# Windowed attention and a low-rank mixer: the same products in another planned order

## The chip, the cores and the metric

The kernel runs on one core of one Trainium2 chip. The metric is device time in microseconds; the kernel before has a median of 240.48 us over 8 runs (239.02 to 241.27). TensorE (PE) multiplies matrices into PSUM, VectorE (DVE), ScalarE (ACT) and GpSimd (POOL) work elementwise, and SyncE (SP) and GpSimd issue transfers (DMA). Each of these executes its own list of instructions in order.

## The reference

```python
# q, k, v: (4, 8, 768, 64); n_global 8, n_local 96
scores = q @ k.T / 8 + bias          # bias = -slope[h] * distance; kept: 0 <= i - j < 96, or j < 8
x = softmax(scores) @ v              # then (4, 768, 512): tokens by channels
u = x + (x.T @ U @ V).T              # mixes tokens through rank 32
out = u + relu(u @ w_ch1) @ w_ch2    # 512 -> 2048 -> 512
```

## The kernel before, in words

The work is cut into 16 **pairs** (batch b of 4, two heads at a time; pair p = 4b + hp) and 4 **mixers**, one for each batch, which follow its four pairs.

A pair is a chain of tasks; the digit after the letters is the pair:

- `lk`, `lq`, `lv` load K, Q and V with a cast to fp16. GpSimd issues them (L393 to L401), except pair 0's K and Q, which SP loads as fp32 and `Ck0`, `Cq0` cast. Three buffers each for K and Q, four for V.
- `TK`, `TQ` transpose K and Q on TensorE (L538) for pairs 0 to 6, evacuated by `EK` (ScalarE) and `EQ`; from pair 7 on `EK` and `EQ` are DMA transposes on SP's queue (L562). `KO` copies the global keys beside each block.
- `VO` makes a copy of V shifted by 32 rows, `VG` adds the global rows. `CFG['VO']` says who shifts: `P`, GpSimd in three copies `VOp.0` to `VOp.2` (L308), for pairs 0 and 1; `S`, one transfer on SP's queue (L589), for all others. `VG` is always GpSimd's.
- `SB` (batch 0 alone) writes the bias into PSUM, `S` adds the scores (L646), in up to three steps; `EX` takes the exponent (ScalarE, L673), `MK` multiplies by a mask (batches 1 to 3; L682, L686).
- `PV` multiplies with V (L734, L735); `RC` and `NM` normalize into `x_sb` (L769, L773); `XC` casts it to fp16 (GpSimd, L799, except for a batch's last pair); `UP` transposes x and multiplies by U (L713, L718); `TE` evacuates the second (L807); `HM` adds the V factor of the mixer (L813); `E0` (for the last pair of a batch `E0` and `E1`) evacuates the sum as one quarter of u, transposed. The last pair of batch 0 does `PV` to `UP` in three parts (`NH` for `NM` and `XC`).

A mixer is 16 steps of `M1a` (three of four quarters of u) and `M1b` (the last) with `RL` (relu, ScalarE, L872) behind them (L855), and then the second product as 7 instead of 8 block products (`P1` to `P7`, L934) for each of three row blocks t: `RS` starts a block (L922), `PA` and `PB` prepare sums of the relu's result on VectorE (L889 to L894), `DI` and `DA` to `DH` gather the results (L947, L970), `O` stores. `w1_0` to `w1_3` and `w2_0` to `w2_3` are quarters of the two weights, loaded once by GpSimd (L443, L452); `TWa` and `TWb` form sums of w2 on VectorE for P4 to P7. `M1a b.n` needs `w1_(n//4)` and u of three pairs.

The order is not written by hand. A `Planner` holds every task with an engine, an assumed duration, a priority, dependencies and buffers, and plays them through: at each step the engine that can start first takes, of its tasks that are ready within a small margin, the one of lowest priority number. The resulting order is then issued; each engine executes its list in that order, waiting where an operand is not there. `PRIO` replaces the priorities of named tasks. Where the plan leaves TensorE a gap ahead of the first mixer, small matmuls on zeros fill it (`idle`, L1005).

Of the kernel before, what the change touches and what calls it, by code (L numbers as in the profile page):

```python
# [16 lines left out]
PE, ACT, DVE, POOL, SP = "PE", "ACT", "DVE", "POOL", "SP"  # L17


PRIO = {  # L20
    "DA0.1": 6761.6, "DB0.1": 7457.2, "DB0.2": 8384.0, "DB1.1": 8060.5, "DB1.2": 7985.3, "DC2.0": 7792.2,
    "DD0.0": 7862.4, "DD0.1": 9270.9, "DD0.2": 8194.4, "DD1.0": 7863.4, "DE0.2": 9402.3, "DF1.2": 9397.4,
    "DG0.0": 8430.4, "DG0.1": 7596.4, "E02": 5865.5, "EQ1": 5461.4, "EQ4": -770.7, "EX13.0": 2425.7,
    "EX7.0": 3812.7, "EX8.0": 3775.7, "HM0": 2046.8, "HM12": 6279.7, "HM4": 6676.8, "HM9": 6950.7,
    "KO2": 5496.8, "KO6": 7318.7, "MK5.1": 9128.9, "NM3": 6024.6, "NM6": 7530.1, "P11.1": 6997.7,
    "P11.2": 1129.7, "P13.0": 1397.9, "P13.1": 5738.6, "P13.2": 5821.2, "P20.1": 6584.3, "P21.2": 7125.0,
    "P22.1": 6477.8, "P22.2": 6901.9, "P31.0": 1661.0, "P31.1": 8414.8, "P31.2": 1130.8, "P32.2": 1563.3,
    "P40.0": 6158.6, "P42.2": 6069.4, "P51.0": 5444.1, "P51.1": 6635.4, "P51.2": 1447.3, "P52.0": 7575.6,
    "P52.2": 6200.8, "P53.0": 6280.2, "P53.1": 6149.2, "P53.2": 6395.6, "P60.1": 1345.9, "P62.0": 6610.3,
    "P62.2": 7609.1, "P63.0": 6108.0, "P63.1": 5480.1, "P63.2": 5772.1, "P70.0": 8347.1, "P70.1": 6738.9,  # L30
    "P70.2": 7027.2, "P71.2": 1364.6, "P72.1": 6440.8, "P73.0": 5851.1, "P73.1": 5567.0, "P73.2": 5452.8,
    "PA0.2": 7917.5, "PV10": 6222.2, "PV4": 6245.6, "PV9": 5349.2, "RS1.1": 6269.9, "RS1.2": 1110.0,
    "RS2.0": 1541.0, "RS2.2": 1422.3, "RS3.1": 5892.6, "RS3.2": 6041.8, "S10.2": 1370.0, "S13.0": 1158.9,
    "S14.2": 6699.6, "S15.2": 6800.7, "S2.0": 1451.2, "S4.0": 7711.3, "S5.2": 6779.7, "S8.0": 5814.4,
    "S9.0": 1264.8, "SB0.0": 1281.0, "TD0": 6084.1, "TE12": 9033.5, "TE4": 7848.7, "TK5": 6104.0,
    "TQ6": 6583.1, "TWa1": 7306.5, "TWb1": 10021.5, "UP10": 1511.1, "UP13": 7260.0, "UP5": 6730.5,
    "UP8": 1455.2, "back": 5375.3, "bias2": 5491.5, "bias5": 5236.3, "bias7": 5097.0, "lk1": -2540.4,
    "lk2": -3457.2, "lk3": -3923.7, "lk4": -38.4, "lk5": 1252.9, "lk6": 1838.7, "lq1": -3379.0,
    "lq2": -3313.7, "lq3": -3230.2, "lq4": -245.4, "lv0": -2414.7, "lv2": -4220.0, "lv4": 502.1,
    "ones0": -3282.3, "ones1": -2613.4, "ones2": -2230.4, "ones3": -2415.2, "vs1": 6166.9, "w1_0": 605.5,  # L40
    "w1_3": 1786.5, "w2_3": 2150.6,
}
CFG = {'petr': (4, 5, 6), 'E': 'DAD', 'VO': 'PPSSSSSSSSSSSSSS'}

# [162 lines left out]
def kernel(  # L207
# [13 lines left out]
    nc = tc.nc  # L221
# [13 lines left out]
    D1 = D + 1  # L235
# [3 lines left out]
    PO = P - 32  # L239
# [6 lines left out]
    def sb(name, shape, dt, n=None):  # L246
        if n is None:
            return cst.tile(shape, dt, name=name)
        return [cst.tile(shape, dt, name=f"{name}{i}") for i in range(n)]
# [9 lines left out]
    vs = sb("vs", [P, 4, HS], FP16)  # L259
# [27 lines left out]
    bias = sA[:, 0]  # L287
# [14 lines left out]
    def copy(eng, dst, src):  # L302
        if eng == ACT:
            nc.scalar.activation(dst, src, AF.Copy)  # L304
        elif eng == DVE:
            nc.vector.tensor_copy(dst, src)
        else:
            nc.gpsimd.tensor_copy(dst, src)  # L308

    def add(eng, dur, prio, fn, deps=(), name="", **kw):  # L310
        return pl.add(name, eng, dur, PRIO.get(name, prio), fn, deps, **kw)
# [32 lines left out]
    c_rel = add(DVE, 2.2, -89, build_rel, [c_id16], name="rel3")  # L344
    c_mask = []

    def bias_of(h, eng):
        def go():
            if eng == ACT:
                nc.scalar.activation(bias[:, h], rel3, AF.Copy, scale=slope[h] / qk_scale)  # L350
            else:
                nc.vector.tensor_scalar_mul(bias[:, h], rel3, slope[h] / qk_scale)
        return go

    c_bias = []
    for h in range(H):
        e = DVE if h in CFG.get("bias_dve", range(H)) else ACT
        c_bias.append(add(e, 0.53 if e == ACT else 0.24, -45 + h if h < 2 else 100 * (h // 2) - 30, bias_of(h, e), [c_rel], name=f"bias{h}"))

    def ones(i):  # L360
        return lambda: nc.gpsimd.memset(vt[i][:, :, :, D:D1], 1.0)
# [114 lines left out]
    def load_mixer():  # L476
# [4 lines left out]
    c_back = add(DVE, 0.07, -44, lambda: nc.vector.memset(uf[0:1, 0, 0:1], 0.0), [c_bias[0]], name="back")  # L481
    c_mixl = add(SP, 0.9, -44, load_mixer, [c_back], size=0.8, parts=2, name="mixl")
    c_u16 = add(
        DVE, 0.95, 10,
        lambda: nc.vector.tensor_copy(u16, uf.unsqueeze(2).broadcast_to((P, NB, RG, R))), [c_mixl], name="u16",
    )

    def build_vs(g):
        def go():
            o, v1, v2 = vs[0:R, g], vf[:, 0:HS], vf[:, HS:S]  # L490
            if g % 2 == 0:
                nc.vector.tensor_copy(o, v2 if g else v1)
            else:
                nc.vector.tensor_tensor(o, *((v2, v1) if g == 1 else (v1, v2)), ALU.subtract)
        return go

    c_vz = add(DVE, 0.5, -95, lambda: nc.vector.memset(vs, 0.0), name="vz")
    c_vs = [add(DVE, 0.5 if g % 2 == 0 else 0.6, 11 + g, build_vs(g), [c_mixl, c_vz], name=f"vs{g}") for g in range(4)]


# [21 lines left out]
    def attention(p):  # L522
        b, hp = pairs[p]
        h0 = 2 * hp
        base = 100 * p
        first = b == 0
        kdur = 0.25
        last = hp == NP - 1
        mg = 0.3 if first else 0.5
        gq, gk, gv, tq, tk, tv = loads[p]  # L530
        gkT, gqT = Group("kT", 2), Group("qT")
        A1, A2 = (ANY1, ANY2) if first else (ATT1, ATT2)
# [35 lines left out]
        if p in by_pe:  # L568
            g1, g2 = Group("ps", among=A1), Group("ps", among=A1)
# [25 lines left out]
        if vm != "S":  # L595
            ve = {"D": DVE, "P": POOL, "A": ACT}[vm]

            def vo_d(c):
                return lambda: copy(ve, vo[gv.slot][c:c + 32], vt[gv.slot][c + 32:c + 64, :, 0:NB - 1])

            VO = [
                add(ve, {POOL: 0.95, DVE: 0.8, ACT: 0.8}[ve], base + 4, vo_d(c), [tv], name=f"VO{p}.{c // 32}") for c in range(0, PO, 32)
            ]
        else:
            VO = [add(SP, 0.6, base + 4, vo_sp, [tv], size=0.6, name=f"VO{p}")]
# [118 lines left out]
        for s in range(3):  # L724
# [12 lines left out]
            if not split:  # L737
# [6 lines left out]
                    rel=[geps[s]] + ([gv] if s == 2 else []), name=f"PV{p}.{s}",  # L744
# [86 lines left out]
        else:  # L831
            e = {"A": ACT, "D": DVE}[CFG.get("E", "DDD")[p] if first else CFG.get("EB", "A")]
# [7 lines left out]
    def mlp(b):  # L840
        base = 100 * NP * (b + 1) + 5000
# [65 lines left out]
        for t in range(ht):  # L907
            gX, gY = Group("ps", 3, among=among), Group("ps", 4, among=among)
            g2, g3 = Group("u2", 2), Group("u3", 1)
# [3 lines left out]
            def half(g, i):  # L913
                return ps[:, g.slot, i * hd:(i + 1) * hd]
# [28 lines left out]
            def dv(eng, dur, fn, dp, nm, **kw):  # L943
                return add(eng, dur, -10, fn, dp, name=f"{nm}{b}.{t}", **kw)

            def plus(e, o, x, y):
                return lambda: e.tensor_tensor(o(), x(), y(), ALU.add)  # L947
# [10 lines left out]
            D1 = dv(DVE, 0.42, plus(V_, lambda g2=g2: u2[g2.slot], lambda gX=gX: half(gX, 1), lambda g2=g2: u2[g2.slot]), [P6, D0], "DA", rel=[gX])  # L958
# [5 lines left out]
            se = POOL if CFG.get("SE", "D") == "P" and not (b == B - 1 and t == ht - 1) else DVE  # L964
# [4 lines left out]
            def both(sn=sn, xy=xy, g2=g2):  # L969
                sn.tensor_tensor(xy, xy, u2[g2.slot].unsqueeze(1).broadcast_to((P, 2, hd)), ALU.add)  # L970

            D5 = dv(se, 1.27 if se == POOL else 0.65, both, [D1], "DE", rel=[g2])
            D6 = dv(DVE, 0.42, plus(V_, lambda x11=x11: x11, lambda gX=gX: half(gX, 0), lambda x11=x11: x11), [P2], "DF", rel=[gX])
            D7 = dv(DVE, 0.42, plus(V_, lambda x21=x21: x21, lambda gY=gY: half(gY, 0), lambda x21=x21: x21), [P4, D5], "DG", rel=[gY])
            D8 = dv(DVE, 0.42, plus(V_, lambda x12=x12: x12, lambda gY=gY: half(gY, 1), lambda x12=x12: x12), [P3, D5], "DH", rel=[gY])

# [10 lines left out]
    for b in range(B):  # L987
        for hp in range(NP):
            if b == 1 and hp == 0:
                c_mask += [  # L990
                    add(
                        ACT, 0.54, 330 + 5 * h,
                        lambda h=h: nc.scalar.activation(mask[:, h], rel3, AF.Exp, scale=slope[h]),
                        [c_rel, pl.names[CFG.get("mask_after", "EX3.1")]], name=f"mask{h}",
                    )
                    for h in range(H)
                ]
            attention(b * NP + hp)
        mlp(b)
# [55 lines left out]
```

The softmax here doesn't subtract the row's maximum and nothing guards it: scores larger than these inputs give would overflow.

## Time and profile before

| | us |
|---|---|
| median of 8 runs | 240.48 |
| the profiled execution | 239.71 |
| its span | 237.9 |
| TensorE busy, all of the span | 226.5 (95%) |
| GpSimd busy | 90.1 (38%) |
| first product of the first mixer starts | 34.76 |
| last matmul ends | 233.92 |
| granted TensorE clock, mean | 0.999 |

A row of the timeline gives start, length, engine, line, operation, tiles and count, and in brackets the idle time ahead of it with what ended it. A row of the stretches gives busy time by engine. "Landing" of a transfer counts from the start of its issue.

### The profile page before, as it was taken

To read this page: it belongs to the slowest core of one execution; us is meant where nothing else is said; L and a number is where in the kernel's file an instruction comes from. 1 tells how busy PE (TensorE), PEld (TensorE's weight loads), DVE (VectorE), ACT (ScalarE), POOL (GpSimd) and SP (SyncE) were. 2 spreads that over 40 slices of the span, in tenths; PEclk is the share of its full clock that TensorE was granted. 3 is DMA by queue.
4 is the path that set the end of the run, shared out by engine and by line. 5 is a ranking of instruction groups with operands and counts; after the bars stand their busy time and mean duration, and the time that the engine had idled before them with its cause. 6 is when DMAs were issued, how large, how long until landed. Compare 5 with 4: busy or idle time off the path is not lost.

```text
span 237.9 us, 5808 instructions
## 1 busy us (share of the span) xinstructions
PE 226.5 (95%) x2436; PEld 165.4 (70%) x2436; DVE 147.5 (62%) x317; ACT 122.8 (52%) x165; POOL 90.1 (38%) x116
## 2 busy tenths in 40 slices
PE   7996989999999999999999999999999999999993
PEld 3653865556888975666888866657889765668872
DVE  6864760548999881656778973465488631537452
ACT  3884955787345246957541358557441225661000
POOL 8759992725959648082074910020001000000000
PEclk9999999999999999999999999999999999999999
DMA  8999699999999999999689999000002220000024
GB/s 178 172 119 130 49 173 197 202 207 187 162 115 155 173 147 170 192 163 132 128 53 162 129 182 174 3 0 0 3 1 91 88 91 2 0 3 0 0 91 176
DMA packets 86442, 26.18 MB, mean 110 GB/s; under 512 B 73840, under 2 KB 83440, under 8 KB 86416
## 3 DMA queue, kind: packets, MB, share of 16 engines
q0 software_dynamic: 63616, 13.24, 70.9%
q1 hardware_dynamic: 22800, 12.57, 25.5%
q8 instruction: 19, 0.31, 0.6%
q14 instruction: 7, 0.06, 0.1%
HBM read 27.46 MB, written 6.29 MB: 142 GB/s over the span
## 4 chain that ended last, share of the span: by engine, by line
PE 81%; DMA 8%; POOL 4%; DVE 3%; issue 1%; SPq 0%; ACT 0%; DVEq 0%; POOLq 0%
PE ps L855 36%; PE ps L934 31%; DMA vt<-in_v_dram 4%; PE ps L646 4%; DMA w<-in_moe_w_ch_dram 3%; PE ps L922 2%; PE ps L735 2%; DMA sA<-in_q_dram 2%; PE ps L713 2%; PE ps L718 2%; PE ps L734 2%; POOL vo L308 2%; PE ps L813 1%; DVE x_sb L947 1%; POOL x L799 1%
## 5 line engine op out<-in xcount | busy, mean ns | idle before, releaser
L855 PE MATMUL ps<-uT,w 128*128 128x384 f16 x512 | 86.4, 327 | 1.5 <-DMA w<-in_moe_w_ch_dram 1.1
L855 PEld LDWEIGHTS <-w 128*128 128x128 f16 x512 | 48.7, 98 | 33.6 <-DMA w<-in_moe_w_ch_dram 1.3
L872 ACT ACTIVATE htr<-ps 128x768 f16<-128x768 f32 x64 | 51.9, 811 | 30.4 <-PE ps L855 30.2
L673 ACT ACTIVATE ep<-ps 128x1024 f16<-128x1024 f32 (+1 forms) x48 | 43.9, 952 | 21.3 <-PE ps L646 21.2
L934 PEld LDWEIGHTS <-htr 128*128 128x128 f16 x384 | 36.6, 98 | 7.0 <-issue 1.5
L934 PEld LDWEIGHTS <-sA 128*128 128x128 f16 x288 | 27.7, 98 | 4.9 <-issue 0.9
L889 DVE TENSOR_TENSOR sA<-htr 128x768 f16<-128x768 f16 x16 | 8.9, 557 | 30.6 <-ACT htr L872 30.6
L401 POOL DMA_DIRECT2D vt<-in_v_dram x16 | 16.8, 1048 | 28.3 <-PE ps L735 24.2
L947 DVE TENSOR_TENSOR x_sb<-ps,x_sb 128x256 f32<-128x256 f32 x48 | 19.4, 419 | 12.8 <-PE ps L934 12.1
L934 PE MATMUL ps<-tB,htr 128*128 128x256 f16 x192 | 24.7, 273 | 1.1 <-DVE x_sb L947 1.0
L934 PE MATMUL ps<-w,sA 128*128 128x256 f16 x192 | 24.5, 273 | 0.8 <-DVE x_sb L947 0.5
L799 POOL CAST x<-x_sb 128x768 f16<-128x768 f32 x12 | 10.8, 898 | 37.8 <-DVE x_sb L773 37.4
L934 PE MATMUL ps<-w,htr 128*128 128x256 f16 x192 | 24.8, 273 | 0.0
L686 DVE TENSOR_TENSOR ep<-ep,mask 128x1024 f16<-128x1024 f16 x24 | 16.9, 706 | 12.5 <-ACT ep L673 12.5
L304 ACT ACTIVATE uT<-ps 128x768 f16<-128x768 f32 (+1 forms) x14 | 10.1, 718 | 26.1 <-PE ps L813 26.1
L308 POOL COPY vo<-vt 32x650 f16<-32x650 f16 x22 | 17.3, 788 | 12.5 <-DMA vt<-in_v_dram 11.9
L397 POOL DMA_DIRECT2D stgq<-in_q_dram x18 | 14.8, 828 | 4.0 <-PE ps L855 2.1
L397 POOL DMA_DIRECT2D stgk<-in_k_dram x18 | 14.8, 832 | 3.2 <-DMA w<-in_moe_w_ch_dram 3.0
L773 DVE TENSOR_TENSOR x_sb<-ps,rcp 128x768 f32<-128x768 f32 x16 | 15.2, 954 | 0.4
L646 PEld LDWEIGHTS <-kT 64*128 64x128 f16 x352 | 9.9, 94 | 7.8 <-issue 6.5
L646 PE MATMUL ps<-qT,kT 64*128 64x128 f16 x352 | 15.2, 218 | 0.0
L947 DVE TENSOR_TENSOR u<-ps,u 128x256 f32<-128x256 f32 x24 | 10.0, 419 | 6.4 <-PE ps L934 5.9
(76 smaller groups left out, 277.2 us busy)
## 6 DMA issues: line engine op xcount, KB each, us to landing
out_dram<-x_sb SPq DMA_DIRECT2D x23, 256.0 KB, 2.7
w<-in_moe_w_ch_dram POOLq DMA_DIRECT2D x8, 512.0 KB, 13.8
vt<-in_v_dram POOLq DMA_DIRECT2D x16, 192.0 KB, 8.5
stgk<-in_k_dram POOLq DMA_DIRECT2D x18, 96.0 KB, 11.2
stgq<-in_q_dram POOLq DMA_DIRECT2D x18, 96.0 KB, 8.5
vo<-vt SPq DMA_DIRECT2D x14, 121.9 KB, 6.1
stgk<-in_k_dram POOLq DMA_DIRECT2D x6, 192.0 KB, 5.5
stgq<-in_q_dram POOLq DMA_DIRECT2D x6, 192.0 KB, 5.6
```

The lines of the kernel that those rows point to most:

```text
L308: nc.gpsimd.tensor_copy(dst, src)
L397: nc.gpsimd.dma_start(o[:, :, hi], src[b, h0 + hi].rearrange("(n p) d -> p n d", p=P))
L401: nc.gpsimd.dma_start(vt[gv.slot][:, :, :, 0:D], v[b, h0:h0 + 2].rearrange("h (n p) d -> p h n d", p=P),)
L646: nc.tensor.matmul(t[:, hi, j * P:(j + 1) * P], lhs, qt[r, i * P:(i + 1) * P], start=not biased, stop=True, skip_group_check=biased,)
L673: nc.scalar.activation(ep[gep.slot][:, :, lo:512], ps[:, gsc.slot:gsc.slot + 2, lo:512], AF.Exp, scale=qk_scale)
L686: nc.vector.tensor_tensor(ev, ev, mv, ALU.mult)
L773: nc.vector.tensor_tensor(xo, pvo()[:, :, :, 0:D], rcp[p % 2].unsqueeze(3).broadcast_to((P, 2, NB, D)), ALU.mult)
L799: (nc.vector if xe == DVE else nc.gpsimd).tensor_copy(x16[gx16.slot], src)
L855: nc.tensor.matmul(ps[:, g.slot + half, 0:HS], w1[:, dc, jt * P:(jt + 1) * P], ub[:, dc, half * HS:(half + 1) * HS], start=(dc == 0), stop ...
L872: nc.scalar.activation(htr[:, jt].rearrange("p (h c) -> p h c", h=2), ps[:, g.slot:g.slot + 2, 0:HS], AF.Relu)
L934: nc.tensor.matmul(o, a[:, j, c0 + cols.start:c0 + cols.stop], bq[:, j], start=False, stop=(j == hj - 1), skip_group_check=True,)
L947: return lambda: e.tensor_tensor(o(), x(), y(), ALU.add)
```

## The change

No task is added or removed. `PRIO` is replaced by another table (about 110 entries before, about 200 after), some assumed durations and margins of the planner are altered, and with them the planned order of every engine. `CFG` is the same; pairs 0 and 1 have V shifted by GpSimd in both kernels.

```diff
 PRIO = {
...
-    "P22.1": 6477.8, "P22.2": 6901.9, "P31.0": 1661.0, "P31.1": 8414.8, "P31.2": 1130.8, "P32.2": 1563.3,
...
+    "P22.1": 652.7, "P22.2": 7861.0, "P23.0": 913.5,
...
-    "UP8": 1455.2, "back": 5375.3, "bias2": 5491.5, "bias5": 5236.3, "bias7": 5097.0, "lk1": -2540.4,
-    "lk2": -3457.2, "lk3": -3923.7, "lk4": -38.4, "lk5": 1252.9, "lk6": 1838.7, "lq1": -3379.0,
...
-    "w1_3": 1786.5, "w2_3": 2150.6,
+    "bias4": 153.0, "bias5": 9143.6, "bias6": 4685.0, "bias7": 3586.0, "lk1": -2848.0, "lk2": -2792.2,
+    "lk3": -1957.8, "lk4": 3473.0, "lk5": 5628.7, "lq1": -2759.1, "lq13": 4852.5, "lq2": -2359.2,
...
+    "vs2": 1567.1, "vs3": 667.9, "w1_0": 1208.4, "w1_1": 6676.3, "w2_0": 5629.2,
 }
...
-        c_bias.append(add(e, 0.53 if e == ACT else 0.24, ...
+        c_bias.append(add(e, 0.53 if e == ACT else 0.28, ...
...
     c_u16 = add(
-        DVE, 0.95, 10,
+        DVE, 0.7, 10,
...
-    c_vz = add(DVE, 0.5, -95, lambda: nc.vector.memset(vs, 0.0), name="vz")
+    c_vz = add(DVE, 0.7, -95, lambda: nc.vector.memset(vs, 0.0), name="vz")
...
-        mg = 0.3 if first else 0.5
+        mg = 0.15 if first else 0.4
...
-                add(ve, {POOL: 0.95, DVE: 0.8, ACT: 0.8}[ve], base + 4, vo_d(c), ...
+                add(ve, {POOL: 0.76, DVE: 0.8, ACT: 0.8}[ve], base + 4, vo_d(c), ...
...
-            D5 = dv(se, 1.27 if se == POOL else 0.65, both, [D1], "DE", rel=[g2])
+            D5 = dv(se, 1.27 if se == POOL else 0.7, both, [D1], "DE", rel=[g2])
```

`mg` is the margin that the planner adds for TensorE to a result of another engine. What the planner makes of it, by the tasks' names in the built programs, up to the middle of the first mixer:

```
GpSimd before  lk3 lk2 lq1 lq2 ones0 ones1 ones3 lv0 lq3 lk1 ones2 lv2 lv1 VO0.0 VO0.1 VO0.2 VG0 VG2 lv3 lk4 lq4 XC0
               VO1.0 VO1.1 VO1.2 VG1 XC2 VG3 lv4 XC1 w1_0 w1_1 w1_2 lk5 lq5 lv5 VG4 w1_3 w2_0 w2_1 w2_2 lk6 lq6 lv6
               VG5 w2_3 lk7 lq7 lv7 VG6 lk8 XC4 lq8
GpSimd after   lk1 lk2 lq1 ones2 lq2 ones0 lv0 lk3 lq3 ones1 lv1 lv2 ones3 lv3 VO0.0 VO0.1 VO0.2 VG0 VO1.0 VO1.1 VO1.2
               VG1 VG2 VG3 w1_0 XC0 XC1 lk4 XC2 lq4 lv4 lk5 w1_1 w1_2 w1_3 w2_0 VG4 w2_1 w2_2 w2_3 lq5 lv5 lk6 lq6 lv6
               XC4 lk7 lq7 VG5 lv7 lk8
TensorE before TK0 TQ0 TK3 SB0.1 SB0.2 TK2 SB0.0 TQ1 S0.0 S0.1 S0.2 TQ2 SB2.0 SB2.1 SB2.2 S2.1 S2.2 TQ3 TK1 S2.0 PV0
               SB1.0 SB1.1 S1.0 S1.1 SB1.2 S1.2 PV2 SB3.0 UP0 S3.0 SB3.1 S3.1 SB3.2 S3.2 HM0 TK4 PV1 TQ4 UP2 PV3.0
               PV3.1 PV3.2 HM2 UP1 HM1 UP3.0 UP3.1 UP3.2 HM3 S4.2 M1a0.0 (M1b0.0 to M1b0.5) M1a0.6 TQ5 ... M1b0.7 TK5
               ... M1b0.9 S4.0 ... M1b0.11 S5.0 ... M1b0.14 TK6 PV4 M1a0.15 M1b0.15 RS0.0 P10.0 RS0.1 P10.1 P20.0 UP4
TensorE after  TK0 TQ0 TK1 SB0.0 TK2 SB0.2 SB0.1 S0.2 TQ1 S0.0 TQ2 S0.1 SB1.0 S1.0 SB1.1 S1.1 TK3 SB1.2 TQ3 S1.2 PV0
               SB2.1 S2.1 SB2.2 SB2.0 S2.2 S2.0 PV1 SB3.0 S3.0 SB3.1 S3.1 PV2 SB3.2 UP0 S3.2 PV3.0 PV3.1 UP1 HM0 UP2
               PV3.2 HM1 HM2 UP3.0 UP3.1 UP3.2 TK4 M1a0.0 HM3 TQ4 M1a0.1 M1b0.0 M1b0.1 S4.0 M1a0.2 TK5 M1b0.2 M1a0.3
               M1b0.3 S4.2 ... M1a0.6 PV4 ... M1b0.8 UP4 ... M1a0.14 TQ5 M1b0.14 M1a0.15 M1b0.15 S5.2 HM4 RS0.2 P10.2
               RS0.0 P10.0 P50.0 S5.0
VectorE after  (first mixer) RC4 NM4 PA0.0 PB0.0 PA0.1 TE4 PB0.1 TWa0 TWb0 TWa1 TWb1 PA0.2 PB0.2 PA0.3 PB0.3
```

The 128-column filling matmuls fall from 76 to 11; the eight of 512 columns at the start stay. Later mixers have the same tasks in another order too: the row blocks of a mixer come in another sequence, `PV` and `UP` of the next batch's pairs earlier or later among them; at the end the last two whole stores are those of `P43.1` and `P33.1`, ahead of the last half store (`P33.2`).

## The prediction

> **What bounds the kernel now.** I read the busy shares by stage first, cut where the first product of the first mixer (M1a0.0) starts; the columns are the stretch, its length, then busy time and instruction count of TensorE, its weight loads, VectorE, ScalarE and GpSimd, the granted clock, DMA share and GB/s.
>
> ```profile
> 0.00:34.76 34.76, 29.59 (x468) 19.70 (x469) 23.52 (x57) 24.31 (x36) 29.64 (x45) 1.00 1.13 135
> 34.76:233.95 199.19, 196.89 (x1968) 145.73 (x1968) 123.25 (x259) 98.52 (x130) 60.49 (x72) 1.00 0.95 105
> ```
>
> From 34.76 us to the last matmul (233.92) TensorE is idle for only 199.16 - 196.89 = 2.27 us. A reordering cannot win more than that there, and can lose much. Ahead of 34.76 the busy 29.59 us hold 84 filling matmuls on zeros (9.2 us by the costliest groups, 3.6 of them before the first operand is there) and count waits that fillers cover. So the profiled execution is 34.76 + 199.16 + 3.98 (last additions and store) = 237.9 us of span, + 1.81 around it = 239.71; the median of the runs, 240.48, is 0.77 above.
>
> Next the timeline of TensorE, where a bracket is a wait and what ended it:
>
> ```profile
> 14.54 0.19 PE L734 MATMUL ps<-vo,ep 128*128 128x65 f16 x1 [0.22 <-POOL vo L308]
> 19.49 0.20 PE L734 MATMUL ps<-vo,ep 128*128 128x65 f16 x1 [1.68 <-DMA vo<-vt]
> 21.17 0.51 PE L713 MATMUL ps<-ident,x 128*128 128x128 f16 x6 [0.58 <-POOL x L799]
> 34.76 8.95 PE L855 MATMUL ps<-uT,w 128*128 128x384 f16 x54 [1.11 <-DMA w<-in_moe_w_ch_dram]
> ```
>
> M1a0.0 waits for the first quarter of w1. Why that is late stands in GpSimd's timeline, then in the landing of the transfer issued at 27.93:
>
> ```profile
> 16.91 0.72 POOL L308 COPY vo<-vt 32x650 f16<-32x650 f16 x1 [2.42 <-DMA vt<-in_v_dram]
> 17.58 1.16 POOL L401 DMA_DIRECT2D vt<-in_v_dram  x1
> 18.73 0.83 POOL L393 DMA_DIRECT2D stgk<-in_k_dram  x1
> 19.54 0.72 POOL L393 DMA_DIRECT2D stgq<-in_q_dram  x1
> 20.30 0.82 POOL L799 CAST x<-x_sb 128x768 f16<-128x768 f32 x1
> 21.18 3.26 POOL L308 COPY vo<-vt 32x650 f16<-32x650 f16 x4
> 24.51 0.82 POOL L799 CAST x<-x_sb 128x768 f16<-128x768 f32 x1
> ...
> 27.16 0.82 POOL L799 CAST x<-x_sb 128x768 f16<-128x768 f32 x1
> 27.93 2.24 POOL L443 DMA_DIRECT2D w<-in_moe_w_ch_dram  x3
> ...
> w<-in_moe_w_ch_dram POOLq DMA_DIRECT2D x1, 512.0 KB, 6.8
> ```
>
> GpSimd is one queue in order. Pair 1's V landed at 18.2 (chain that ended last: 9.55 + 8.67), but its shift (VO1, VG1) starts at 21.18 behind three load issues and a cast; PV1 runs at 24.84, its cast at 27.16, and only then is w1 issued: 27.93 + 6.8 = 34.7.
>
> **The change, part by part.** All edits act through the planner; instructions and tiles stay, except fillers. The shift of V by GpSimd for pairs 0 and 1 stands in both kernels; only its planned price changes.
>
> *Work moved across the border.* HM3, TQ4 and S4.2 now follow M1a0.0. The chain prices them 0.33 (L813 x2), 0.46 (L538 x12), 0.33 (L646 x8): 196.9 + 1.1 = 198.0 us of product work behind the start.
>
> *Fillers.* 65 of the 76 small ones go (6 take 0.50 us with their drain). They ran inside waits, so I credit nothing. Their cover is the clock. The clock row is 1.00 in both stretches, and the 1.68 us wait at 19.49 did not lower it. [...] The longest wait that I get below is 2.4 us. [...]
>
> *First stage.* I walk GpSimd's new order with the durations above (k issue 0.87, q 0.71, V 1.06 to 1.16, ones 0.2, four shifts 3.1 to 3.3). lk1 lk2 lq1 lq2 lv0 lk3 lq3 lv1 lv2 lv3 from 1.58 end at 12.0, against 10.6 for the last of lv1 and lv2 before: lv3 moved ahead, at the price of VO0. VO0, VG0: 12.0 to 15.1 (11.4 to 14.5 before), so PV0 is 0.6 late; behind it pair 2's scores. lv1 is now tenth in the transfers; the tenth landed at 8.44 + 8.4 = 16.9, and lv2 then at 18.2. VO1, VG1: 16.9 to 20.1, so PV1 at 20.15 instead of 24.84. VG2, VG3 to 21.6; w1_0 issued 21.6 instead of 27.93; XC0 to 23.2, XC1 to 24.1, lk4 to 24.9, XC2 to 25.7.
>
> TensorE: pair 2's scores end about 17.7, then it waits for PV1 (the 2.4 us); 20.15 PV1, SB3.0 S3.0 SB3.1 S3.1 to 22.2, PV2 (its V by transfer: 18.2 + 2.5) to 22.8, SB3.2 23.3, UP0 to 24.0, S3.2 24.3; ScalarE's EX3.2 (1.02) ends at 25.4, against 25.1. So pair 3's scores gain nothing: UP0 stands ahead of S3.2 and waits for XC0, which waits behind the shifts. The gain is behind it: UP1 to 25.4, UP2 (XC2) to 26.4, PV3.2 26.65, HM1 and HM2 to 27.5, while VectorE does E00 to 26.8, TE2, RC3.2, NH3.0, NH3.2 to 28.1 and E02 (0.95) to 29.05. M1a0.0 needs E02, and TK4 stands just ahead of it: lk4, issued 24.1, landed after 5.3 before, 29.4 here if it is not held by w1_0. [...] M1a0.0 starts at **29.6**; ends 28.7 (only E02) and 32 (a late lk4, or VO1 a microsecond or two late).
>
> *Supply inside M1.* Landings before, as issue plus time to landing: w1_0 34.7, w2_3 60.2. In these 25.5 us ran seven weight pieces and the loads of pairs 5 and 6 (6.85 us between their landings): (25.5 - 6.85)/7 = 2.66 a piece, back to back. New: lk4 lq4 lv4 lk5 land to 33.0 (lk5 issued 27.6, plus 5.3), then w1_1 35.7, w1_2 38.3, w1_3 41.0, w2_0 43.6 and w2_3 51.6. M1a0.4 needs w1_1 at 37, so w1 is in time. Two steps behind it may not be.
>
> First UP4. It is moved up, from after RS0.1 P10.1 P20.0 to right behind M1b0.8; on GpSimd its cast XC4 stands behind lv6. Before, each load of this stretch was issued as the eighth before it landed (w2_2 at 38.04 after w1_1's 37.75, lk7 at 46.49 after w1_3's 46.2). So lv6 waits for w2_0: 43.6 + 0.3 + 1.03, XC4 0.83, end 45.8. TensorE reaches UP4 at 29.6 + 9 x 1.31 (six products of 0.327 for two thirds, two for the rest) + 2.7 (HM3, TQ4, S4.0, TK5, S4.2, PV4) + 0.3 (small waits for lq4 and for a bank) = 44.4. It waits **1.5**; ends 0, and 2.9 if the four pieces take the 3.0 us of w1_1 and w1_2 before. Behind it in TensorE's queue is every later product; who waits for those is ScalarE's relu.
>
> Then TQ5, which needs lq5. That load now follows all of w2: landing 51.6 + 1.0 = 52.6, where it was 42.4. TensorE comes there at 45.9 + 5 x 1.31 + 0.98 + 0.67 = 54.1. No charge; 0 to 1.9.
>
> VectorE has TWa0 to TWb1 between PB0.1 and PA0.2, so PA0.2 waits for w2_3: 51.6 + 2.8 (four of 0.69), then PA0.2, PB0.2, PA0.3 (1.2, 1.1, 1.2) = 57.9. P50.0, which needs PA0.3, is reached at 54.1 + 0.46 + 0.33 + 1.31 + 0.66 + 2.6 = 59.5. No charge; the cover is 1.6 us, and beyond it each microsecond counts.
>
> *Later batches.* The order inside them is new; the 2.27 us of waits of before mostly stand where an addition is followed at once by its product. I keep 1.2 of it, ends 0 and 4.
>
> *Sum.* 29.6 + 198.0 + 0.3 + 1.5 + 1.2 = 230.6 to the last matmul; tail 4.2 (3.98, and 0.2 as two whole stores now come just ahead of the last half one): span 234.8, + 1.8 = 236.6, + 0.8 to the median: **237.4**, 3.1 us under 240.48.
>
> **Rivals.** *All waits vanish*, as w2_0 comes by 42: start 29.0, waits 1.0: 29.0 + 198.0 + 1.0 + 4.2 + 2.6 = 234.8. For it: the loads ahead of w1 are out of its way by about 19. Against it: pieces never came faster than 2.2 us apart. [...] *The start hardly moves*, since pair 3's scores do not: at 32 the wait at UP4 vanishes with it and only 0.9 is lost; at 34 it is 2.9, 240.3, no change. For it: EX3.2 ends no earlier. Against it: in the kernel before, everything behind PV1 hung on VO1. *The supply takes the gain back:* UP4 waits 3.5 and the later batches lose 2.5: 240.7, no change. For it: transfers are busy at 9 tenths from 28 us on. *Slower:* XC4 behind lv6 alone. Each microsecond by which w2_0 lands after 43.6 is one of idle TensorE, as nothing else may pass UP4. It decides from a wait of 5.8 (1.5 + 4.3, 241.7), w2_0 at 47.9, which is 3.7 us a piece from 33.0 on; at 4.0 it ends at 242.8. Against it: no piece of before took more than 3.05. *The change does nothing:* excluded, since the queues stand in another order.
>
> **How the numbers follow.** Forecast as summed 0.57 (its own range 235.8 to 239.2), waits vanish 0.12, clock 0.04, start at 34 0.08, supply 0.11, slower 0.08. Half a per cent (1.2 us) is about what a measurement of this kernel can tell, so faster means below 239.3, slower above 241.7. Faster: 0.52 + 0.12 + 0.02 + 0.01 + 0.02 = 0.69. Same: 0.05 + 0.02 + 0.05 + 0.06 = 0.18. Slower: 0.02 + 0.03 + 0.08 = 0.13. The range leaves out about 0.1 on each side: 234.6 to 241.6, from waits gone to the supply's worse end.
>
> **What would show it.** First product near 29.6, w1's first issue near 21.6, VO1 starting at its landing near 16.9, PV1 near 20; TensorE waiting 1 to 3 us at L713 inside M1 for GpSimd's cast L799; TQ5 without a wait; the clock row at 1.00. It is wrong if M1a0.0 starts after 32, if TensorE idles over 5 us behind it, or if the later batches lose more than they did.

## The result and the profile after

The changed kernel takes 238.17 us (median of 20 runs, 237.1 to 240.63) against 240.11 us for the kernel before beside it (57 runs, 238.06 to 242.23): a ratio of 0.9925, 95% interval 0.9905 to 0.9945. It is faster by 0.75%, inside the range, 0.8 us above the forecast of 237.4. The profiled execution took 238.63 us with a span of 236.9, so it lies 0.46 above its kernel's median, where that of before (239.71) lies 0.40 below. The two traces therefore differ by 1.1 us, of the 1.9 between the medians. Ratios leave out executions that took over 1.5% more than the fastest of their kernel; medians have all of them.

Every execution has its mean granted clock on record. A stretch at half clock, which lasts 3.41 us in the trace below (47.33 to 50.74 us), takes 0.7% off that mean (0.993 in the profiled execution, with one such stretch), and the time behind the last matmul up to 0.4% (0.989 in the second trace of this kernel, with one stretch too), so the mean tells about how many there were. The executions by that count, with the median time of each group (the kernel before in the runs beside the experiments):

| | no stretch (clock 0.996 or more) | one (0.987 to 0.995) | two (0.984 or less) |
|---|---|---|---|
| before, 51 executions | 32: 239.78 us | 19: 241.32 us | none |
| changed, 21 executions | 5: 237.37 us | 12: 238.31 us | 4: 239.67 us |

By these groups the change is worth 2.4 us at full clock. The changed kernel loses the clock more often, and gives back 0.5 us of it between the medians.

The program has 17 more lines ahead of the tasks: L713 is now L730, L734 is L751, L799 is L816, L855 is L872. First the page of the changed kernel, TensorE's busy tenths and granted clock and the transfers in 40 slices of 5.9 us:

```profile
PE   7987989599999999999999999999989999999993
...
PEclk9999999979999999999999999999999999999999
DMA  8992999999999999929692993400003030000114
```

There are three things to see. TensorE has a hole in the eighth slice (41 to 47 us). Its clock falls in the ninth, right behind that hole. And the transfers have a hole of their own in the fourth slice (18 to 24 us), early in the kernel, when there is still much to load.

The stretches of the changed kernel, in the columns of the prediction, cut at M1a0.0, at the start and end of the wait ahead of UP4, and at the end of the slow clock:

```profile
0.00:29.03 29.03, 25.54 (x382) 15.40 (x382) 22.06 (x54) 21.24 (x32) 25.84 (x40) 1.00 1.22 141
29.03:44.85 15.82, 15.14 (x145) 8.89 (x142) 6.82 (x14) 11.86 (x17) 8.20 (x11) 1.00 1.35 196
44.85:47.50 2.65, 0.00 (x0) 0.00 (x0) 1.36 (x3) 0.81 (x1) 1.85 (x2) 0.97 1.24 207
47.50:51.00 3.50, 3.50 (x20) 2.38 (x21) 1.96 (x5) 0.00 (x0) 1.21 (x2) 0.54 1.25 206
51.00:59.50 8.50, 8.50 (x63) 4.88 (x61) 6.71 (x11) 5.56 (x7) 6.30 (x8) 1.00 2.09 173
59.50:233.10 173.60, 172.62 (x1769) 130.59 (x1768) 108.28 (x232) 83.39 (x109) 46.77 (x56) 1.00 0.74 90
```

Behind M1a0.0 TensorE is busy for 15.14 + 0 + 3.50 + 8.50 + 172.62 = 199.76 us and idle for 4.3, so the last matmul ends at 29.03 + 199.76 + 4.3 = 233.1. Before, it ended at 233.92. A start 5.73 us earlier has moved the end by 0.8. The fourth row holds one of the reasons: 3.50 us at a granted clock of 0.54 are work for 1.9 us at full speed, so 1.6 us are lost to the clock. The last row holds the later batches, with 0.98 idle.

TensorE's timeline of the changed kernel says what the idle time ended on:

```profile
15.22 0.19 PE L751 MATMUL ps<-vo,ep 128*128 128x65 f16 x1 [0.60 <-POOL vo L325]
19.70 0.19 PE L751 MATMUL ps<-vo,ep 128*128 128x65 f16 x1 [1.43 <-POOL vo L325]
29.03 1.14 PE L872 MATMUL ps<-uT,w 128*128 128x384 f16 x6
31.09 0.53 PE L555 MATMUL ps<-ident,stgq 128*64 128x128 f16 x12 [0.60 <-DMA stgq<-in_q_dram]
47.50 0.82 PE L730 MATMUL ps<-ident,x 128*128 128x128 f16 x6 [2.65 <-POOL x L816]
57.31 0.53 PE L555 MATMUL ps<-ident,stgq 128*64 128x128 f16 x12
```

PV0 and PV1 (the two rows of L751) start near 15 and 20, and M1a0.0 at 29.03 has no bracket: it no longer waits for w1. UP4 (L730) waits 2.65 us for the cast XC4. TQ5 (57.31) does not wait. The length of UP4 is part of the clock's price: its six matmuls take 0.82 us, and 0.51 where the clock is full.

GpSimd's timeline of the changed kernel, from the shifts of V to that cast:

```profile
12.10 3.07 POOL L325 COPY vo<-vt 32x650 f16<-32x650 f16 x4
16.37 5.27 POOL L325 COPY vo<-vt 32x650 f16<-32x650 f16 x6 [1.20 <-DMA vt<-in_v_dram]
21.59 0.75 POOL L460 DMA_DIRECT2D w<-in_moe_w_ch_dram  x1
...
30.26 0.80 POOL L469 DMA_DIRECT2D w<-in_moe_w_ch_dram  x1
...
41.76 0.70 POOL L410 DMA_DIRECT2D stgq<-in_q_dram  x1 [1.66 <-DMA w<-in_moe_w_ch_dram]
45.55 1.03 POOL L418 DMA_DIRECT2D vt<-in_v_dram  x1 [3.09 <-DVE sA L911]
46.63 0.82 POOL L816 CAST x<-x_sb 128x768 f16<-128x768 f32 x1
```

The shifts of pairs 1 to 3 now run as one block as soon as pair 1's V is there (16.37), and w1's first quarter is issued at 21.59. At the bottom the chain that costs the most: w2_0 is issued at 30.26 and lands near 45.0, lv6 is issued at 45.55, the cast stands behind it and ends at 47.45, and UP4 starts at 47.50. The bracket of lv6 names VectorE, but the issue follows w2_0's landing by half a microsecond, and below, where w2_0 lands earlier, lv6 is issued earlier with it.

### The profile page after: what moved, and what is told of

Same layout as the page of the kernel before. It is cut to its first block, busy times and chain, and to the rows that moved or that the text cites. A ratio compares the mean times of both kernels' runs of the same rounds, so it can differ in the third digit from the quotient of the medians.

```text
span 236.9 us, 5670 instructions
## 1 busy us (share of the span) xinstructions
PE 225.3 (95%) x2371; PEld 162.1 (68%) x2371; DVE 147.6 (62%) x317; ACT 122.9 (52%) x165; POOL 90.2 (38%) x116
## 4 chain that ended last, share of the span: by engine, by line
PE 80%; DMA 8%; POOL 7%; issue 3%; DVE 1%; ACT 0%; POOLq 0%; DVEq 0%
PE ps L951 32%; PE ps L872 31%; DMA w<-in_moe_w_ch_dram 5%; PE ps L663 4%; DMA vt<-in_v_dram 3%; PE ps L939 2%; POOL vo L325 2%; PE ps L730 2%; PE ps L752 2%; PE ps L830 2%; PE ps L735 2%; PE ps L1022 2%; PE ps L751 1%; POOL x L816 1%; POOL w L460 1%
## 5 line engine op out<-in xcount | busy, mean ns | idle before, releaser
L872 PE MATMUL ps<-uT,w 128*128 128x384 f16 x512 | 88.3, 329 | 0.1
L872 PEld LDWEIGHTS <-w 128*128 128x128 f16 x512 | 48.9, 98 | 32.2 <-issue 1.0
L690 ACT ACTIVATE ep<-ps 128x1024 f16<-128x1024 f32 (+1 forms) x48 | 44.4, 952 | 20.3 <-PE ps L663 19.7
L816 POOL CAST x<-x_sb 128x768 f16<-128x768 f32 x12 | 10.6, 891 | 43.7 <-DVE rcp L786 25.0
L703 DVE TENSOR_TENSOR ep<-ep,mask 128x1024 f16<-128x1024 f16 x24 | 16.4, 687 | 15.3 <-ACT ep L690 15.3
L906 DVE TENSOR_TENSOR sA<-htr 128x768 f16<-128x768 f16 x16 | 9.0, 562 | 21.8 <-ACT htr L889 21.6
L321 ACT ACTIVATE u<-ps 128x256 f32<-128x256 f32 x12 | 4.6, 383 | 27.1 <-PE ps L951 19.5
L663 PE MATMUL ps<-qT,kT 64*128 64x128 f16 x352 | 15.8, 218 | 0.0
## 6 DMA issues: line engine op xcount, KB each, us to landing
vo<-vt SPq DMA_DIRECT2D x14, 121.9 KB, 4.8
```

The costliest lines, as they stand in the source:

```text
L663: nc.tensor.matmul(t[:, hi, j * P:(j + 1) * P], lhs, qt[r, i * P:(i + 1) * P], start=not biased, stop=True, skip_group_check=biased,)
L690: nc.scalar.activation(ep[gep.slot][:, :, lo:512], ps[:, gsc.slot:gsc.slot + 2, lo:512], AF.Exp, scale=qk_scale)
L703: nc.vector.tensor_tensor(ev, ev, mv, ALU.mult)
L816: (nc.vector if xe == DVE else nc.gpsimd).tensor_copy(x16[gx16.slot], src)
L872: nc.tensor.matmul(ps[:, g.slot + half, 0:HS], w1[:, dc, jt * P:(jt + 1) * P], ub[:, dc, half * HS:(half + 1) * HS], start=(dc == 0), stop ...
```

## The experiments

The kernels are edits of the changed kernel or of the one before. An order is edited behind the planner, so nothing else moves. In all of them each named task is taken out and put in behind another:

```diff
     order = pl.run()
+    part = [pl.names[n] for n in MOVED]
+    order = [t for t in order if t not in part]
+    at = order.index(pl.names[BEHIND]) + 1
+    order[at:at] = part
```

Added fillers are 128-column matmuls on zeros into a bank that is free there:

```diff
+            if t.name == NAME:
+                idle(COUNT, P, BANK)
             if t.eng == PE:
```

No experiment leaves work out.

### Is the wait at UP4 the load ahead of its cast?

Changed kernel, MOVED lv6, BEHIND XC4.

> The changed kernel with one load moved on GpSimd's queue: lv6 is issued behind XC4 instead of ahead of it. Theory (UP4 waits for XC4, XC4 for lv6, lv6 for w2_0, and the clock falls behind that wait): the wait of 2.65 us at L730 is gone, the clock row stays at 1.00, so 2.65 + 1.6 us are won, less up to 0.7 at TQ5, whose load lands at 53.7: span 233.0 to 233.6, ratio to the kernel before about 0.978. Rival (transfers are the bound, the wait only moves): TensorE waits as long at TQ5 or at P50.0, span within 1 us of 236.9.

Measured: 235.86 us, ratio 0.9824 (0.9786 to 0.9861), span 234.3. UP4 starts at 45.96 without a wait. From 18 to 62 us TensorE's timeline has two waits of 0.3 us or more, at PV1 and, for VectorE's `tB`, at TQ5:

```profile
20.50 0.19 PE L751 MATMUL ps<-vo,ep 128*128 128x65 f16 x1 [1.88 <-POOL vo L325]
54.77 0.53 PE L555 MATMUL ps<-ident,stgq 128*64 128x128 f16 x12 [0.51 <-DVE tB L524]
```

So one load issue ahead of one cast held TensorE. The wait did not move elsewhere, so the rival is wrong. The span is 0.7 us longer than the theory had, which took the clock to stay full. Here it fell behind the wait at PV1 (the column ahead of the last two is the clock):

```profile
20.00:22.00 2.00, 1.50 (x22) 1.01 (x21) 1.21 (x3) 0.05 (x1) 2.00 (x3) 0.69 0.36 98
22.00:24.00 2.00, 2.00 (x17) 0.71 (x16) 1.08 (x2) 0.81 (x1) 1.96 (x4) 0.50 0.24 9
```

M1a0.0 starts at 30.97 in it, 1.9 later than in the trace of the changed kernel. The waits at PV1 differ by 0.45, and (2.0 x 0.31) + (2.0 x 0.50) = 1.6 us at most go to the clock.

The two orders were run again beside each other, with what was expected of each:

> The changed kernel itself, unaltered, beside the next three on the same chip, as their base: ratio 0.992 to 0.993 as before; UP4 waits 2 to 3 us, with a slow stretch of the clock behind it.

> lv6 behind XC4, once more, beside its base. Theory (wait at UP4 and the clock behind it are 4.2 us, less a wait for lq5 and, in some executions, a slow stretch behind PV1): 1.0 to 1.5 per cent below the changed kernel. Rival (the earlier difference was partly of the chip): less than 0.6 per cent below it.

The changed kernel took 238.28 (0.9894, 0.9834 to 0.9955), the edited one 235.67 (0.9798, 0.9754 to 0.9842). The slowest of the six runs of the edited kernel, 236.44, is under the fastest of the six of the changed one, 236.97. By the ratios the load ahead of the cast costs 1.0%, 2.3 us. Among executions with the same clock it costs 2.6, which is the wait alone: 237.0 against 234.37 where the clock stayed full (two executions and one), 238.28 against 235.70 where it fell once (two and five). The clock's part of the 4.2 us that were expected did not come, since the edited order loses the clock at PV1. In the second trace of the changed kernel, UP4's wait was longer than in the first:

```profile
20.30 0.21 PE L751 MATMUL ps<-vo,ep 128*128 128x65 f16 x1 [1.87 <-POOL vo L325]
48.86 0.51 PE L730 MATMUL ps<-ident,x 128*128 128x128 f16 x6 [2.96 <-POOL x L816]
```

Its six matmuls take 0.51 us: behind this wait of 2.96 us the clock did not fall. It fell behind the 1.87 at PV1.

### What is the clock worth?

Changed kernel, 44 fillers ahead of UP4, so that TensorE has work while it waits.

> The changed kernel with 44 matmuls on zeros (128 columns, into the bank that UP4 then overwrites) just ahead of UP4, so that TensorE works through the wait for XC4. Theory (the slow 3.4 us behind the wait are the clock, halved after an idle window): UP4 still starts at about 47.5, its matmuls and the next ones run at full clock, 1.6 us are won: span 235.3. Rival (they are slow because of the transfers that run at that time, or the first matmuls behind any wait are): the span stays at 236.9.

Measured: 237.46, ratio 0.9894 (0.9861 to 0.9928), span 235.6. UP4 starts where it did, and the clock is full; the first row is UP4, the second the stretch behind it:

```profile
47.74 0.51 PE L730 MATMUL ps<-ident,x 128*128 128x128 f16 x6 [0.42 <-POOL x L816]
```

```profile
47.50:51.00 3.50, 3.26 (x28) 2.25 (x29) 1.82 (x4) 0.81 (x1) 1.17 (x3) 1.00 1.25 208
```

The span is 1.3 us under that of the changed kernel, though UP4 is 0.24 later: 1.3 to 1.6 us are the clock's part of that execution. The slow matmuls were the clock, and not the transfers, which are as busy as before (1.25 and 208 GB/s here, 1.25 and 206 there). The medians (238.17 and 237.46) agree with it in sign, but the intervals of their ratios overlap, since the clock does not fall in every execution. With the fillers it stayed full in 7 of 12 executions (median 237.33), without them in 5 of 21 (237.37): at full clock the two kernels take the same time.

The same at the other wait: MOVED lv6, BEHIND XC4, and 28 fillers ahead of PV1.

> The run with lv6 behind XC4, and 28 matmuls on zeros (1.6 us) ahead of PV1, into the bank that PV1 then overwrites, to cover its wait for VO1. In the profile of the run without them the clock was halved for some 4 us behind a wait of 1.9 us at PV1, in the changed kernel (1.4 us) it was not. Theory (that stretch of slow clock is a second cost of the same kind, though it comes in some executions only): the clock row stays at 1.00 throughout, span 233.3, and the ratio to the kernel before falls from 0.982 to 0.978 or below. Rival (the slow stretch lies beside other work in the first stage and costs nothing): the ratio stays at 0.982.

> lv6 behind XC4 and 28 matmuls on zeros ahead of PV1, beside the same without them. Theory (the slow stretch behind PV1's wait costs 1 to 1.5 us where it comes): 0.3 to 0.5 per cent below the run without them. Rival (it lies beside other work): the same.

Measured: 234.94 (0.9789, 0.9749 to 0.9829, span 232.6) and, run again, 234.99 (0.9784, 0.974 to 0.9829, span 233.3), with mean clocks of 0.999. Beside the second run ran the same order without these fillers, at 235.67: 0.3% more, inside the intervals. Its profiled execution had a full clock by itself, so that these two traces do not differ in what was to be told apart. The clocks of all executions do: without the fillers the clock fell in 8 of 12 (median 235.78, and 234.88 in the other four), with them in 1 of 12 (234.77 in the other eleven). So the fillers keep the clock, and are worth some 0.9 us in an execution that would have lost it. The rival is wrong. The ratios fall with the fillers (0.9824 to 0.9789, 0.9798 to 0.9784), but within their intervals.

### Is the early start worth anything?

Changed kernel, 36 fillers (2.0 us) ahead of M1a0.0.

> The changed kernel with 36 matmuls on zeros (2.0 us of added work) between TK4 and M1a0.0, in the bank that M1a0.0 waits for. Theory (up to UP4 the time is set by the landing of w2_0 and not by TensorE): UP4 still starts at 47.5, after a wait of 0.6 to 0.8 instead of 2.65, too short to lower the clock: span 235.3, faster than without the added work. Rival (TensorE's own work sets it): 2.0 us longer, span 238.9.

Measured: 237.85, ratio 0.9908 (0.9876 to 0.994), span 235.6. The rival, in which the microseconds ahead of the mixer count, is excluded: it needed a ratio of about 1. M1a0.0 started at 32.48, 3.45 us later than in the changed kernel (2.0 of fillers; the rest was PV1's wait, 1.87, and 3.4 us of half clock behind it). Yet UP4 is just as far:

```profile
32.48 0.81 PE L872 MATMUL ps<-uT,w 128*128 128x384 f16 x4
...
47.77 0.51 PE L730 MATMUL ps<-ident,x 128*128 128x128 f16 x6
```

It starts 0.27 us later than in the changed kernel, and with no bracket. A start that was 3.45 us earlier had been turned into a wait of 2.65 us, and into the slow clock behind it. As long as UP4 stands behind w2_0's landing, the gain of the first stretch stops there.

### What makes w2_0 late?

Changed kernel, w1_0 moved into the hole of the transfers: MOVED w1_0, BEHIND VG0 (issued at 15.04), and MOVED w1_1, BEHIND VG3, w1_0's old place.

> The changed kernel with w1_0 issued behind VG0 (15.2 instead of 21.6) and w1_1 at w1_0's old place. Theory (a weight quarter in the transfers holds up V's shift by transfer, as in the kernel before with w1_0 moved to 15.1, where VO2 took 6.2 us instead of 2.5): VO2 and VO3 land late, PV2 waits 2 us or more behind PV1, M1a0.0 starts at 31 or later, the wait at UP4 vanishes since w2_0 comes some 2 us earlier: span 236 to 238. Rival (supply is what counts, V is shifted in time): M1a0.0 stays at 29, no wait at UP4, span 233.

Measured: 235.38, ratio 0.9799 (0.9757 to 0.984), span 233.8. Neither UP4 nor TQ5 waits. The theory of a wait at PV2 is wrong, the rival that the supply counts is right: V's two copies took 3.3 us by their median (2.6 before the edit), and PV2 stands behind PV1 in this order, which came later anyway. The stretch from 18 to 20 us of the changed kernel, and then of the edited one, shows the transfers (the last two columns are their share and GB/s):

```profile
18.00:20.00 2.00, 0.57 (x16) 0.44 (x13) 2.00 (x4) 1.71 (x2) 1.94 (x3) 1.00 0.28 70
```

```profile
18.00:20.00 2.00, 0.20 (x4) 0.10 (x3) 2.00 (x3) 1.63 (x2) 1.90 (x3) 0.98 1.29 215
```

In this stretch 215 GB/s are moved instead of 70. The pieces behind come earlier: w2_0 is issued at 30.87 and lands after 12.1 us, at 43.0 instead of 45.0, lv6 is issued at 43.46 instead of 45.55, and XC4 is out of TensorE's way even behind it. M1a0.0 started at 30.71, as PV1 waited 2.21 us and the clock fell at that wait.

### Which part of the start is w1's place, and which the shift of V?

Kernel before, MOVED w1_0, BEHIND VG0 and, in a second kernel, BEHIND VG3 (issued at 25.49 instead of 27.93).

> The kernel before with one transfer moved: w1_0 is issued right behind VG0, in GpSimd's idle time at 14.5, instead of behind XC1 at 27.9. Theory (w1 was late by 1.1 us only, the first stage hung on pair 1's V): M1a0.0 starts at 33.7 instead of 34.8 and the span falls by 1.1 to 236.8, ratio 0.995. Rival (the late issue of w1 held the first stage): M1a0.0 starts near 30, the span falls by 4 or more.

> The kernel before with w1_0 issued behind VG3 (at 26.1 instead of 27.9, ahead of lv4 and XC1). It asks again what w1's place alone is worth, where no shift of V is under way. Theory (1.1 us at most, since pair 1's chain ends just ahead of it, and XC1 is 0.75 later now): M1a0.0 at 34.0 to 34.6, span 237.1 to 237.7, no change by the ratio. Rival (w1's late issue held the first stage): M1a0.0 starts 1.8 us earlier, span 236.1, ratio 0.992 or less.

The first took 243.26, ratio 1.0136 (1.0096 to 1.0176): slower, which neither theory had. The SP transfer of pair 2's V in the window from 16 to 20 us, in the kernel before and then with the load ahead of it (last column: us from issue to landing):

```profile
vo<-vt SPq DMA_DIRECT2D x1, 121.9 KB, 2.5
```

```profile
vo<-vt SPq DMA_DIRECT2D x1, 121.9 KB, 6.2
```

Here PV2 stands ahead of PV1 and of pair 3's scores, so TensorE waits for that copy, and works at half clock from 21.3 to 28.1:

```profile
23.09 0.24 PE L734 MATMUL ps<-vo,ep 128*128 128x65 f16 x1 [4.55 <-DMA vo<-vt]
```

```profile
22.00:24.00 2.00, 0.91 (x17) 0.91 (x18) 0.00 (x0) 0.00 (x0) 1.90 (x3) 0.50 1.53 170
```

M1a0.0 started at 38.66. The same load at the same place (there with w1_1 moved up as well) gained 1.3% on the changed kernel and lost 1.4% here. In this order a product stands in line for the copy that took 6.2 us. In the other none did, and the earlier supply took away the wait at UP4.

The second took 239.39, ratio 0.9968 (0.994 to 0.9996), with M1a0.0 at 33.66 and no wait at it. That is the upper end of what the theory gave, and the rival's larger gain did not come. So w1's earlier issue alone is worth 1.1 us of the start (34.76 to 33.66), just the 1.11 us that M1a0.0 had waited. The other 4.6 us (33.66 to 29.03) came with the rest of the order. VO1 at its landing and 1.1 us of work moved behind are what the traces name for it; neither was tried alone, so how the 4.6 us divide is not shown.

### Is the shift of pair 1's V by GpSimd in the way?

Changed kernel, MOVED lv6, BEHIND XC4; pair 1's V shifted by one SP transfer instead of GpSimd's three copies; 14 fillers ahead of PV1.

```diff
+    pl.names['VO1.0'].fn = by_transfer[1]
+    for n in ('VO1.1', 'VO1.2'):
+        pl.names[n].fn = lambda: None
```

> The run with lv6 behind XC4, and pair 1's V shifted by one transfer on SP's queue instead of three copies on GpSimd; 14 matmuls on zeros ahead of PV1. What it shows is what the shift by GpSimd is worth in the new order. Theory (VO1 on GpSimd holds PV1 and, behind it, w1_0 and the casts, by 2.3 us of copies): VO1 lands near 19.3, w1_0 is issued near 19.8, PV1 at 19.4 at the latest, M1a0.0 at 28.2: span 232.5 to 233.3. Rival (the transfers are full until 19 with V itself, so that the shift by transfer takes over 4 us, and VO2 and VO3 queue behind it): PV1 after 20.5, span above 234.3.

Measured: 234.51, ratio 0.9777 (0.974 to 0.9813). It is not told apart from the order with GpSimd's copies (234.94 beside it). The transfer, issued at 16.59, is used at 20.36, where the three copies had PV1 start at 20.02 in the kernel beside it:

```profile
20.36 0.20 PE L753 MATMUL ps<-vo,ep 128*128 128x65 f16 x1 [1.47 <-DMA vo<-vt]
```

GpSimd issues w1_0 at 20.22 here, 1.4 us earlier than in the changed kernel, and nothing comes of it.

### All edits together

Changed kernel, w1_0 and w1_1 as in the order with the early load, lv6 behind XC4, 28 fillers ahead of PV1.

> The three edits together: w1_0 behind VG0 and w1_1 at its old place, lv6 behind XC4, 28 matmuls on zeros ahead of PV1. Theory (with the start kept warm and lq5 landing 2 us earlier, the wait at TQ5 goes too): M1a0.0 at 29.2, span 232.2, ratio to the kernel before 0.976. Rival (w1 holds up V's shift by transfer, and what is won at TQ5 is lost at PV2): as lv6 behind XC4 with the matmuls on zeros, 0.979, or worse.

Measured: 234.83, ratio 0.9775 (0.9731 to 0.9818), span 232.8, full clock, M1a0.0 at 30.07, no wait at UP4 or TQ5. That is 1.2% under the changed kernel beside it by the two ratios, and 2.2% under the kernel before, and no better than lv6 behind XC4 with fillers (234.99): the early load and the moved load heal the same wait, and it can be healed once. Of the versions tried, moving lv6 alone is the smallest edit that beats both kernels (235.86 and 235.67).

## Why the prediction was right, and where it was off

**Start.** Right, by its own steps. VO1 started at 16.37 (16.9), PV1 at 19.70 (20.15), w1_0 was issued at 21.59 (21.6), M1a0.0 started at 29.03 (29.6). TensorE waited 1.43 us at PV1 (2.4), as pair 2's scores ended later, at 18.27 (17.7). w1_0 took 5.3 us to land (6.8 in the trace of before), and was there at 26.9. That w1 was the last thing awaited before was right too; its part alone is 1.1 us. What the early start was worth as long as UP4 waits for w2_0 is another matter: of its last 3.45 us, nothing.

**Work behind the start.** Busy 199.76 at the end, less 1.6 of clock: 198.2 (198.0).

**UP4.** Mechanism right, size off: 2.65 us, not 1.5, and inside the bounds of 0 to 2.9. TensorE reached it at 44.85 (44.4). lk5 landed at 33.35 (33.0). The mis-sized term is the time of a weight piece: the four up to w2_0 (45.0) took (45.0 - 33.35)/4 = 2.9 us each and not 2.66. The mean of 2.66 mixed slow pieces with fast ones, which its own upper bound (3.0) had named; here too the first four were slower, and w2_1 to w2_3 then landed at 47.55, 50.15 and 52.7, 2.6 apart.

**Fillers and clock.** This is the step that failed. The forecast counts no time for the clock, by one row: a wait of 1.68 us behind which the clock stayed at 1.00. The trace of the changed kernel lost 1.6 us to the clock, behind a wait of 2.65. The row was one wait in one execution, and it tells nothing of the next: in the traces the clock fell behind waits of 1.87, 1.88 and 2.21 us, and did not behind 2.03, 2.05 and 2.96. In 16 of the 21 executions the clock fell at least once, and a fall cost some 0.9 us of time. The forecast gives a drop of the clock a chance of 0.04. No run ahead of it shows the price that goes with this chance; what the runs showed is 1.6 us in one trace, and the 0.9 between the medians. Nor was the price 0 in the kernel before: in 19 of its 51 executions the clock fell, for 1.5 us. Whether it falls more often now for the fillers that are gone or for the new wait at UP4 was not tried apart in full; fillers at UP4 raised the full executions from 5 of 21 to 7 of 12.

**Small terms.** The wait for lq4 was 0.60 (0.3 for small waits). The later batches kept 0.98 of waits (1.2). TQ5 and P50.0 cost nothing, as said. The tail was 3.8 (4.2).

**The sum.** Last matmul 233.1 instead of 230.6: start -0.6, clock +1.6, UP4 +1.15, small waits and rounding +0.3. The profiled time was 238.63 and not 236.6, 2.0 off. The median was only 0.8 off because the 0.8 added to get from a profiled execution to the median turned out as -0.46. That was luck, and it hid the clock twice: the trace of before had a full clock, so that by the table above the 0.8 between it and the median lay in the clock of other executions, and the trace of the changed kernel had a fall in it. Without the clock the sum closes: 236.6 - 0.6 + 1.15 + 0.3 = 237.45, where the executions at full clock took 237.37. The gain at full clock closes too: 5.73 us of earlier start, less 1.1 of moved work, 2.0 of added waits (4.3 against 2.27) and 0.2 of longer busy time, is 2.4.

**Rivals.** "The start hardly moves" said that a start at 32 would lose only 0.9, as UP4's wait would vanish with it. The late start bears that out: at 32.48 the wait was gone. The supply did not take the whole gain back (UP4 3.5 in that rival, 2.65 here).

## What to carry to other kernels

When a change lets an engine come sooner to a place, ask what it will wait for there: here 3.45 us of earlier start were worth nothing until one load issue was moved off the path of one small cast. In an in-order queue that also issues loads, a cast that the main engine needs belongs ahead of a load that has to wait until an earlier one has landed (1.0% here). A single execution whose clock stayed full behind a wait (1.68 us, in the trace of before) is not a price of zero for the next wait (1.6 us lost behind 2.65, in the trace of the changed kernel); carry the clock's cost with a chance, compare executions of equal clock, and look at where the transfer engines stand idle before moving a load earlier (a share of 0.28 from 18 to 20 us here).

## What the hardware showed that I had not expected

**The clock.** In these traces TensorE's granted clock fell to half at waits of 1.87 (twice), 1.88, 2.21, 2.65 and 4.55 us. It did not at waits of 1.43, 1.47, 1.68, 1.84, 2.03, 2.05 and 2.96. So the length of the wait does not sort them, and the same instruction of the same program did both (UP4 at 2.65 and 2.96, PV1 at 1.88 and 2.05). The fall at UP4 lasted 3.41 us; the others lasted 3.4 by their rows of the clock, and twice that, 6.8, at the wait of 4.55. So one execution says little of the price: over 21 executions of the changed kernel the clock never fell in 5, fell once in 12 and twice in 4. What else decides it was not tried by an experiment.

**Transfers.** A small copy within the core's memory (121.9 KB) went from 2.5 to 6.2 us when half a megabyte of weights was issued just ahead of it from another engine. In the other order the same load cost V's copies 0.7 us (3.3 instead of 2.6).
